# An early load of the exp table and an order guard for score steps, in a fused attention and gated-MLP kernel

## The chip, the cores and the metric

The kernel runs on one core of a Trainium2 chip. The metric is the device time of one execution in microseconds (us).

The core has a matrix engine (TensorE; PE in the profile, PEld for its weight loads), a vector engine (VectorE, DVE), an engine for activation functions and copies (ScalarE, ACT), a general engine (GpSimd, POOL), and SyncE (SP), which here issues most of the DMAs (transfers between memories).

## The reference, cut to what matters

Two layers run on the same normalised input, and both are added to it: a sliding-window attention (2048 tokens, 32 heads of 16, window 256) and a gated MLP whose gate mixes tokens with a 2048 x 2048 matrix.

```python
xn = layernorm(x)
# A: attention over a window
qkv = xn @ wqkv
scores = einsum('bhqd,bhkd->bhqk', q, k) * 16 ** -0.5     # masked to 0 <= i - j < 256
o = softmax(scores) @ v
A = o @ wo
# B: gated MLP
z = gelu(xn @ w_in);  z1, z2 = halves of z
g = w_sp @ layernorm(z2) + b_sp                            # mixes tokens
B = (z1 * g) @ w_out
return x + A + B
```

## The kernel before

It has two phases. Phase one computes `z` (a gelu on ScalarE) and 39 of 48 "QKV units", each four matmuls into one PSUM bank (PSUM is the memory that this kernel's matmuls write into) and one copy out of it. Phase two does the other nine QKV units, and then interleaves on TensorE: score steps (`S`), token mixing (`gf`), attention times V (`o`) and the output projections (`fo`). ScalarE takes the exp of each score step. The order of phase two is made at build time by a small loop that keeps estimates of the time on each engine; each engine gets its own list of instructions in that order.

The end of phase one:

```python
    for n in range(NB):
        ...                              # z_half(n, 0), z_half(n, 1) with gelu, and 3 QKV units
    r = z_stats(NB - 1)
    z_apply(NB - 2, r)
    z_apply(NB - 1, r)
    nc.vector.tensor_copy(out=b_all[:], in_=b_bf[:])
```

The loop of phase two:

```python
while ...:
    now = est["pe"]
    if si < len(groups):
        gk, us_ = groups[si]
        if not qq and not s_third and kind != "q" and q_end + 0.3 <= now:
            third_s()                    # QKV's PSUM banks become a third score buffer
        free = set_end[2 * si - (2 if s_third else 1)] + 0.1 if si >= 1 else 0.0
        if free <= now and not qq and (us_[-1] < NE or pv_done > us_[-1] - NE):
            end = do_scores(gk, us_)     # score matmuls, and their exps on ScalarE
            ...
            continue
    ...
    if cur is None:
        cur, kind = pick()               # "q": the next QKV unit, while there are any
    c = next(cur)                        # issues one matmul of the current work
    ...
```

`qq` is empty as soon as the last QKV unit has been picked, so a score step may be issued in the middle of that unit.

A V unit is copied to a staging tile and scattered by four DMAs, all issued by SyncE:

```python
    st = stg.tile([P, 2, H // 2, DH], BF, name="vst", bufs=3)
    (nc.vector.tensor_copy if n % 2 else nc.scalar.copy)(out=st[:], in_=...)
    for e in range(2):
        for kk in range(2):
            nc.sync.dma_start(out=v_bd[e * KB : (e + 1) * KB, v_at(2 * n + kk, e), :, :],
                              in_=st[kk * KB : (kk + 1) * KB, e, :, :])
```

The exps go into three large tiles `E` in turn. The first two have their own space; the third takes the space of the QKV pools, which close first:

```python
def e_tile(u):
    i = u % NE                           # NE = 3
    if i not in E_sb:
        E_sb[i] = Et = (ep if i < 2 else late()).tile([P, EW], BF, ...)   # late() closes the QKV pools
        nc.vector.memset(Et[...], 0.0)   # two memsets of the columns between the rows
```

The softmax here doesn't subtract the row's maximum and nothing guards it: scores larger than these inputs give would overflow.

Of the kernel before, what the change touches and what calls it, by code (L numbers as in the profile page):

```python
# [11 lines left out]
ACT = mybir.ActivationFunctionType  # L12
# [29 lines left out]
def kernel(  # L42
# [12 lines left out]
    nc = tc.nc  # L55
# [18 lines left out]
    warm = pers.tile([P, 8], F32, name="warm")  # L74
# [62 lines left out]
    def load_wsp(t):  # L137
        wspT[t] = wspp.tile([P, NB, P], BF, name="wspT")
        nc.sync.dma_start_transpose(out=wspT[t][:], in_=B_w_sp[t * P : (t + 1) * P, :])
# [14 lines left out]
    with ExitStack() as actx:  # L154
# [23 lines left out]
        with nc.allow_non_contiguous_dma(reason="tiny bias gather"):  # L178
# [3 lines left out]
            out=w_out_sb[:, 0:5, :], in_=B_w_out[0:640, :].rearrange("(c p) n -> p c n", p=P)  # L182
# [31 lines left out]
        def setup_late():  # L214
            mt = lt.tile([P, 2, P], BF, name="mt", bufs=1)
            nc.gpsimd.memset(mt[:], 1.0)
            nc.gpsimd.affine_select(
                out=mt[:, 0, :], in_=mt[:, 0, :], pattern=[[1, P]], compare_op=ALU.is_ge,
                fill=0.0, base=0, channel_multiplier=-1,
            )  # L220
            nc.gpsimd.affine_select(
                out=mt[:, 1, :], in_=mt[:, 1, :], pattern=[[-1, P]], compare_op=ALU.is_gt,
                fill=0.0, base=0, channel_multiplier=1,
            )
            for i in range(3):
                for e in range(2):
                    r = slice(e * KB, (e + 1) * KB)
                    nc.gpsimd.tensor_copy(out=mACA[r, i, :], in_=mt[r, i % 2, r])
# [11 lines left out]
        def rstd(mvt, k):  # L240
            ve = sm.tile([P, 4], F32, name="ve")
            rs = sm.tile([P, 4], F32, name="rs")
            nc.vector.tensor_scalar(  # L243
                out=ve[:, 0:k], in0=mvt[:, 0:k, 1], scalar1=LN_EPS, scalar2=None, op0=ALU.add
            )
            nc.gpsimd.tensor_tensor(  # L246
                out=rs[:, 0:k], in0=ve[:, 0:k], in1=mhalf[:, 0:k], op=ALU.pow
            )
            return rs

        def ln_batch(b0, k):
            mvt = sm.tile([P, 4, 2], F32, name="mvt")
            for n in range(b0, b0 + k):
                ln_stats(n, b0, mvt)
                if n == b0 + k - 1:
                    rs = rstd(mvt, k)
                    for m in range(b0, b0 + k):
                        rsx[m] = rs[:, m - b0 : m - b0 + 1]
                yield
# [10 lines left out]
        def transposes(n, xn):  # L270
            if n >= 8:
                nc.sync.dma_start_transpose(out=xnT[:, :, n * P : (n + 1) * P], in_=xn[:])
                return
            tp = psum["f"].tile([P, NC, P], BF, name="tp", tag="f")
            for c in range(NC):
                nc.tensor.transpose(  # L276
                    out=tp[:, c, :], in_=xn[:, c * P : (c + 1) * P], identity=ident[:]
                )
            nc.scalar.copy(out=xnT[:, :, n * P : (n + 1) * P], in_=tp[:])  # L279

        def z_half(n, half):
            zp = ps_s.tile([P, 2, 512], F32, name="zp", tag="S")
            for c in range(NC):
                for j in range(2):
                    f0 = half * FH + j * HALF
                    nc.tensor.matmul(  # L286
                        zp[:, j, 0:HALF],
                        lhsT=xnT[:, c, n * P : (n + 1) * P],
                        rhs=w_in_sb[:, c, f0 : f0 + HALF],
                        start=(c == 0), stop=(c == NC - 1),  # L290
                    )
            dst = (z1 if half == 0 else z2n)[:, n, :]
            nc.scalar.activation(  # L293
                out=dst.rearrange("p (j f) -> p j f", j=2),
                in_=zp[:, :, 0:HALF], func=ACT.Gelu_apprx_tanh,
            )
# [3 lines left out]
        def z_stats(n):  # L300
            if n % 2 == 0:
                zmv[n // 2] = sm.tile([P, 4, 2], F32, name="zmv")
            mvt = zmv[n // 2]
            st = sm.tile([P, 2, nc.vector.BN_STATS_DIM], F32, name="st2")
            for j in range(2):
                nc.vector.bn_stats(out=st[:, j, :], in_=z2n[:, n, j * HALF : (j + 1) * HALF])
            nc.vector.bn_aggr(out=mvt[:, n % 2, :], in_=st[:])
            if n % 2 == 1:
                return rstd(mvt, 2)
            return None  # L310
# [24 lines left out]
        for n in range(NB):  # L335
            b, j = divmod(n, 4)
            z_half(n, 0)
            if n == 0:
                transposes(1, xns.pop(1))
            elif n == 6:  # L340
                setup_late()
            elif n in (9, 10):
                load_wsp(n - 9)
            if b < 3:
                if j < 2:
                    for _ in ln_batch(4 * b + 4 + 2 * j, 2):
                        pass
                if 1 <= j < 3:
                    for m in range(2):
                        k = 4 * b + 4 + 2 * (j - 1) + m  # L350
                        xns[k] = ln_apply(k)
                        if k >= 8:
                            transposes(k, xns.pop(k))
            if n >= 1:
                r = z_stats(n - 1)
                if r is not None:
                    z_rs[n - 1] = r
            if n >= 3:
                for _ in qkv_unit(*qkv_list.pop(0)):
                    pass  # L360
            z_half(n, 1)
            if n == 0:
                transposes(2, xns.pop(2))
            elif n == 1:
                transposes(3, xns.pop(3))
                setup_early()
            if n % 2 == 1 and n >= 3:
                r = z_rs[n - 2]
                z_apply(n - 3, r)
                z_apply(n - 2, r)  # L370
            if n >= 3:
                for _ in range(2):
                    for _ in qkv_unit(*qkv_list.pop(0)):
                        pass
            if b == 0 and j >= 2:
                for m in range(2):
                    k = 4 + 2 * (j - 2) + m
                    transposes(k, xns.pop(k))
        r = z_stats(NB - 1)
        z_apply(NB - 2, r)  # L380
        z_apply(NB - 1, r)
# [5 lines left out]
    def third_s():  # L387
        o_ctx.close()
        psum.pop("o")
        s_third.append(  # L390
            ctx.enter_context(tc.tile_pool(name="ps_s3", bufs=1, space=bass.MemoryType.PSUM))
        )
# [255 lines left out]
    qq = list(qkv_list)  # L648
# [3 lines left out]
    cur = None  # L652
# [24 lines left out]
    kind = None  # L677
    while si < len(groups) or mask_q or pv_q or qq or gq or fq or cur is not None:
# [3 lines that stand above are left out]
            if not qq and not s_third and kind != "q" and q_end + 0.3 <= now:  # L682
                third_s()
            free = set_end[2 * si - (2 if s_third else 1)] + 0.1 if si >= 1 else 0.0
            if free <= now and not qq and (
                us_[-1] < NE or pv_done > us_[-1] - NE
            ):
                end = do_scores(gk, us_)
                if gk != "R1":
                    for u in us_:  # L690
                        mask_q.append((end + 0.1, (u, gk), (gk in "TQ") == (u % 2 == 0)))
                si += 1
                continue
        while mask_q and mask_q[0][0] <= now:
            t0, m, fin = mask_q.pop(0)
            dur = do_mask(*m)
            est["dve"] = max(est["dve"], t0) + dur
            if fin:
                pv_q.append((est["dve"] + 0.2, divmod(m[0], NG)))
        if cur is None:  # L700
            if evac[-4 if qq else -2] + 0.1 > now:
                est["pe"] = now + 0.05
                continue
            cur, kind = pick()
            if cur is None:
                est["pe"] = now + 0.05
                continue
        c = next(cur)
        if c > 0:
            est["pe"] += c  # L710
        else:
            evac.append(-c)
            est["pe"] += 0.1
            if kind == "q":
                q_end = max(q_end, -c)
            if kind == "pv":
                pv_done += 1
            if kind == "f":
                f_done += 1
            cur = None  # L720
# [27 lines left out]
```

## Time and profile before

| | value |
|---|---|
| median time, 20 runs | 274.36 us (273.38 to 276.06) |
| span in the profile | 271.9 us |
| TensorE busy | 264.3 us, 97% |
| ScalarE busy | 198.9 us, 73% |

The page of the kernel before: the span, the busy time of each engine, and the engines' shares of the chain of work that ended last.

```profile
span 271.9 us, 8363 instructions
...
PE 264.3 (97%) x3565; PEld 160.7 (59%) x3565; DVE 153.9 (57%) x421; ACT 198.9 (73%) x268; POOL 35.8 (13%) x80
...
PE 92%; DMA 3%; ACT 1%; DVE 1%; SPq 1%; issue 0%; ACTq 0%
```

TensorE does nearly everything on the chain. A busy share of 97% says that little idle time is left to win, and says nothing of where it lies. So look for holes. Adding up the gaps between TensorE's records gives 3.07 us in the first 20 us, 1.05 us between 80 and 92 us, and none after that. The hole between 80 and 92 us is where phase one becomes phase two. The view of waits names it (who waited for what: us in total, times, longest):

```profile
PE S L592 <- ACT E_1139 L613: 0.9, 2, 0.6
```

TensorE in order of time there (start, duration, engine, line, operation, tiles, count, idle time and what ended it):

```profile
77.58 1.33 PE L286 MATMUL zp<-w_in_sb,xnT 128*128 128x344 bf16 x8
...
87.67 0.38 PE L100 MATMUL pj_f<-xnT,wqkv 128*128 128x512 bf16 x1
87.98 0.37 PE L592 MATMUL S<-qT,kpad 32*128 32x192 bf16 x8
88.28 0.82 PE L100 MATMUL pj_f<-xnT,wqkv 128*128 128x512 bf16 x3
88.94 1.48 PE L468 MATMUL gf<-z2n,wspT 128*128 128x344 bf16 x9
90.73 0.20 PE L592 MATMUL S<-qT,kpad 32*128 32x64 bf16 x2 [0.32 <-ACT E_1139 L613]
91.54 0.34 PE L592 MATMUL S<-qT,kpad 32*128 32x64 bf16 x14 [0.60 <-ACT E_1139 L613]
91.82 1.34 PE L468 MATMUL gf<-z2n,wspT 128*128 128x344 bf16 x8
```

Read it downwards. 77.58 is the last group of matmuls for `z`; **this moment is called z0 below**. At 87.67 the last QKV unit has issued one matmul, then score step 0 is pushed in (87.98), then come the other three. Score step 1 should follow nine `gf` matmuls at about 90.3. Its first two matmuls wait until 90.73 and the rest until 91.54, each for an exp. ScalarE in the same window tells why:

```profile
87.87 0.59 ACT L106 CAST qT<-pj_o 128x512 bf16<-128x512 f32 x1 [1.39 <-PE pj_o L100]
88.47 1.28 ACT L613 ACT_TABLE_LOAD   x1
89.76 1.73 ACT L613 ACTIVATE E_1139<-S 128x896 bf16<-128x896 f32 x2
91.38 0.59 ACT L109 CAST kst<-pj_f 128x512 bf16<-128x512 f32 x1
...
94.37 0.92 ACT L613 ACTIVATE E_1142<-S 128x896 bf16<-128x896 f32 x1
95.27 0.92 ACT L613 ACTIVATE E_1322<-S 128x896 bf16<-128x896 f32 x1
```

The first exp finds the gelu table loaded. The load takes 1.28 us and pushes both exps back, and the copy of the last K unit (`kst`) stands behind them. Line 95.27 is the first exp into the third E tile (`E_1322`). VectorE, at that time, prepares this tile:

```profile
94.94 0.27 DVE L419 MEMSET E_1322<- 128x256 uint32 x1 [0.65 <-DMA v_bd<-vst]
```

That memset had waited for the last V scatter DMA, which landed at 94.73.

### The profile page before, as it was taken

To read this page: it belongs to the slowest core of one execution; us is meant where nothing else is said; L and a number is where in the kernel's file an instruction comes from. 1 tells how busy PE (TensorE), PEld (TensorE's weight loads), DVE (VectorE), ACT (ScalarE), POOL (GpSimd) and SP (SyncE) were. 2 spreads that over 40 slices of the span, in tenths; PEclk is the share of its full clock that TensorE was granted. 3 is DMA by queue.
4 is the path that set the end of the run, shared out by engine and by line. 5 is a ranking of instruction groups with operands and counts; after the bars stand their busy time and mean duration, and the time that the engine had idled before them with its cause. 6 is when DMAs were issued, how large, how long until landed. Compare 5 with 4: busy or idle time off the path is not lost.

```text
span 271.9 us, 8363 instructions
## 1 busy us (share of the span) xinstructions
PE 264.3 (97%) x3565; PEld 160.7 (59%) x3565; DVE 153.9 (57%) x421; ACT 198.9 (73%) x268; POOL 35.8 (13%) x80
## 2 busy tenths in 40 slices
PE   6899999999999899999999999999999999999994
PEld 2665555555554466666665675757566666766651
DVE  7796947945456365646545555665556465522222
ACT  7576565565564999999999999999999999200000
POOL 6222412101101011010101010101010101101110
PEclk9999999999999999999999999999999999999999
DMA  7983231664201248462909276539162448456621
GB/s 231 389 214 118 59 67 32 119 84 105 45 21 32 48 68 169 96 132 50 140 12 176 45 108 78 110 33 154 40 150 44 105 70 119 101 116 145 145 70 59
DMA packets 73078, 27.84 MB, mean 102 GB/s; under 512 B 62944, under 2 KB 71568, under 8 KB 73040
## 3 DMA queue, kind: packets, MB, share of 16 engines
q1 hardware_dynamic: 71312, 23.10, 43.9%
q0 software_dynamic: 1440, 3.93, 4.8%
q8 instruction: 28, 0.46, 0.7%
q10 hardware_dynamic: 288, 0.26, 0.3%
q14 instruction: 10, 0.08, 0.1%
HBM read 8.41 MB, written 2.10 MB: 39 GB/s over the span
## 4 chain that ended last, share of the span: by engine, by line
PE 92%; DMA 3%; ACT 1%; DVE 1%; SPq 1%; issue 0%; ACTq 0%
PE gf L468 28%; PE o L539 14%; PE zp L286 13%; PE fo L496 8%; PE S L592 6%; PE fo L502 5%; PE pj_f L100 4%; PE pj_o L100 4%; DMA w_in_sb<-in_B_w_in_dram 3%; PE pj_f L119 2%; PE pj_o L119 2%; DMA v_bd<-vst 1%; ACT E_1139 L613 1%; PE tp L276 0%; SPq L162 0%; DVE xo L507 0%
## 5 line engine op out<-in xcount | busy, mean ns | idle before, releaser
L468 PE MATMUL gf<-z2n,wspT 128*128 128x344 bf16 x512 | 84.9, 310 | 0.0
L468 PEld LDWEIGHTS <-wspT 128*128 128x128 bf16 x512 | 46.0, 97 | 25.5 <-issue 2.4
L286 PE MATMUL zp<-w_in_sb,xnT 128*128 128x344 bf16 x256 | 42.2, 309 | 1.4 <-DMA w_in_sb<-in_B_w_in_dram 1.4
L474 DVE SCALAR_TENSOR_TENSOR u<-gf,b_all,z_61 128x344 bf16<-128x344 f32 x32 | 18.4, 576 | 38.7 <-PE gf L468 31.3
L613 ACT ACTIVATE E_1142<-S 128x1024 bf16<-128x1024 f32 (+3 forms) x43 | 36.5, 871 | 0.3
L613 ACT ACTIVATE E_1139<-S 128x1024 bf16<-128x1024 f32 (+3 forms) x43 | 35.4, 848 | 0.1
L286 PEld LDWEIGHTS <-xnT 128*128 128x128 bf16 x256 | 24.9, 98 | 16.7 <-ACT xnT L279 0.8
L613 ACT ACTIVATE E_1322<-S 128x1024 bf16<-128x1024 f32 (+3 forms) x39 | 33.6, 923 | 0.2
L592 PE MATMUL S<-qT,kpad 32*128 32x256 bf16 (+3 forms) x648 | 30.1, 230 | 0.9 <-ACT E_1139 L613 0.9
L509 POOL DMA_DIRECT2D out_dram<-xo x14 | 7.7, 548 | 146.8 <-DVE xo L507 146.8
L592 PEld LDWEIGHTS <-kpad 32*128 32x128 bf16 x960 | 14.1, 92 | 18.3 <-issue 17.4
L496 PE MATMUL fo<-w_out_sb,uT 128*128 128x512 bf16 x96 | 24.4, 379 | 0.0
L111 DVE TENSOR_SCALAR kpad<-kst,hmask 128x512 bf16<-128x512 bf16 x32 | 9.8, 350 | 24.7 <-ACT kst L109 24.6
L507 DVE TENSOR_TENSOR xo<-fo,xo 128x512 bf16<-128x512 f32 x16 | 11.1, 692 | 22.0 <-PE fo L502 22.0
L246 POOL TENSOR_TENSOR rs<-ve,mhalf 128x2 f32<-128x2 f32 (+1 forms) x18 | 12.4, 689 | 64.7 <-DVE ve L243 64.7
L293 ACT ACTIVATE z2n<-zp 128x688 bf16<-128x688 f32 x16 | 11.9, 745 | 11.1 <-PE zp L286 11.1
L293 ACT ACTIVATE z_61<-zp 128x688 bf16<-128x688 f32 x16 | 11.9, 746 | 10.9 <-PE zp L286 10.9
L100 PEld LDWEIGHTS <-wqkv 128*128 128x128 bf16 x128 | 12.4, 98 | 11.8 <-issue 0.2
L619 DVE TENSOR_TENSOR E_1142<-E_1142,mACA 128x512 bf16<-128x512 bf16 (+1 forms) x32 | 15.3, 504 | 4.9 <-ACT E_1142 L613 4.7
L502 PE MATMUL fo<-wo_sb,oT 128*128 128x512 bf16 x64 | 17.3, 380 | 0.0
L100 PE MATMUL pj_f<-xnT,wqkv 128*128 128x512 bf16 x64 | 16.6, 379 | 0.0
L619 DVE TENSOR_TENSOR E_1139<-E_1139,mACA 128x512 bf16<-128x512 bf16 (+1 forms) x31 | 14.5, 496 | 3.6 <-ACT E_1139 L613 3.5
(225 smaller groups left out, 372.4 us busy)
## 6 DMA issues: line engine op xcount, KB each, us to landing
v_bd<-vst SPq DMA_DIRECT2D x64, 32.0 KB, 1.9
xo<-in_A_x_dram POOLq DMA_DIRECT2D x16, 128.0 KB, 3.3
out_dram<-xo POOLq DMA_DIRECT2D x14, 128.0 KB, 2.8
wqkv<-in_A_wqkv_dram SPq DMA_DIRECT2D x1, 1536.0 KB, 11.3
w_in_sb<-in_B_w_in_dram SPq DMA_DIRECT2D x2, 688.0 KB, 6.3
w_out_sb<-in_B_w_out_dram SPq DMA_DIRECT2D x1, 640.0 KB, 6.2
xt_101<-in_A_x_dram SPq DMA_DIRECT2D x1, 512.0 KB, 7.9
xt_102<-in_A_x_dram SPq DMA_DIRECT2D x1, 512.0 KB, 12.1
```

The lines of the kernel that those rows point to most:

```text
L100: nc.tensor.matmul(pt[:], lhsT=wqkv[:, c, w0 : w0 + P], rhs=xnT[:, c, t0 : t0 + 512], start=(c == 0), stop=(c == NC - 1),)
L246: nc.gpsimd.tensor_tensor(out=rs[:, 0:k], in0=ve[:, 0:k], in1=mhalf[:, 0:k], op=ALU.pow)
L286: nc.tensor.matmul(zp[:, j, 0:HALF], lhsT=xnT[:, c, n * P : (n + 1) * P], rhs=w_in_sb[:, c, f0 : f0 + HALF], start=(c == 0), stop=(c == NC ...
L293: nc.scalar.activation(out=dst.rearrange("p (j f) -> p j f", j=2), in_=zp[:, :, 0:HALF], func=ACT.Gelu_apprx_tanh,)
L468: nc.tensor.matmul(gf[:, 0:HALF], lhsT=wspT[t][:, c, :], rhs=z2n[:, c, j * HALF : (j + 1) * HALF], start=(c == 0), stop=(c == NB - 1),)
L474: nc.vector.scalar_tensor_tensor(out=u[:, j * HALF : (j + 1) * HALF], in0=gf[:, 0:HALF], scalar=b_all[:, t : t + 1], in1=z1[:, t, j * HALF ...
L496: nc.tensor.matmul(fo[:], lhsT=uTs[t][:, ch, :], rhs=w_out_sb[:, ch, :], start=(ch == 0), stop=False,)
L502: nc.tensor.matmul(fo[:], lhsT=oTs[t][:, c, :], rhs=wo_sb[:, c, :], start=False, stop=(c == NC - 1),)
L539: nc.tensor.matmul(o[:, q, s, :], lhsT=Et[:, col : col + P], rhs=v_bd[:, v_at(kb, 0) : v_at(kb, 1) + 1 : kb + 1, 4 * G + s, :], start=(i = ...
L592: nc.tensor.matmul(S[s // 2][:, s % 2, col : col + n * KB], lhsT=kpad[32 * s : 32 * s + 32, G, kb, :, :].rearrange("p e k -> p (e k)"), rh ...
L613: nc.scalar.activation(out=dst, in_=src, func=ACT.Exp, scale=SM_SCALE)
L619: nc.vector.tensor_tensor(out=ap, in0=ap, in1=m.unsqueeze(1).to_broadcast([P, ap.shape[1], 2, KB]), op=ALU.mult,)
```

## The change

The intent: load the exp table while ScalarE has time, directly behind the last gelu, by an exp of four numbers that nobody uses; and let no score step into a QKV unit that is being issued, so that ScalarE's copy for that unit isn't put behind exps.

```diff
@@ end of phase one @@
+        nc.scalar.activation(out=warm[:, 0:4], in_=warm[:, 4:8], func=ACT.Exp)
         r = z_stats(NB - 1)
@@ the loop of phase two @@
-            if free <= now and not qq and (
+            if free <= now and not qq and (cur is None or kind != "q") and (
                 us_[-1] < NE or pv_done > us_[-1] - NE
             ):
```

The built kernels differ on TensorE in one place only: the eight matmuls of score step 0 stand behind the last unit's four instead of behind its first. On ScalarE the load and the dummy exp come after a V copy, and the last K copy comes before the first exps. As the loop's estimates moved too, the third score buffer opens one step earlier, at step 1. From there to the end the order of TensorE's work is the same.

## The prediction

> **What bounds the kernel now.** TensorE: 264.3 of 271.9 us busy, 92% of the chain that ended last (page, parts 1 and 4). From 92 us on it never idles (gaps between its records: 3.07 us in the first 20 us, 1.05 from 80 to 92, then none). ScalarE is 9 tenths full from 92 to 236 us, but follows: score steps find their buffer freed 0.15 to 0.6 us earlier, and exps start 0.03 to 0.25 us after the scores end (timeline). So only the hole at the transition can be saved.
>
> **That hole (timeline, 79 to 99 us).** Score step 0 stands after the first matmul of the last QKV unit. ScalarE reaches it at 88.47: exp table load 1.28 us, two exps from 89.76, then the last K copy (91.38). Step 1 needs both score buffers, as the third is not open yet: TensorE idles 0.32 us at 90.41 and 0.60 at 90.94 (wait view: S on E_1139, 0.9); against back-to-back issue, 0.39 + 0.80 = 1.19 us.
>
> **What the change does (instruction order of the built kernels).** (a) Table load and dummy exp (the pair took 1.28 + 0.21 us for gelu at the start) move to about 81.3 us, behind a V copy. Two copies end 1.3 us later, at about 83.3 and 83.9; their PSUM banks are wanted at 83.9 and 84.8, and VectorE takes the K copy only at 84.71: no cost. No later load remains. The Trainium skill ("ScalarE: Activation LUTs", What ACT_TABLE_LOAD costs) gives 1283 ns plus a 1380 ns drain; this trace shows the 1283 but no drain: the copy before ends at 88.46, the exp starts at 89.76. (b) Step 0 follows the last unit's four matmuls, so the K copy precedes the exps, and the third score buffer opens one step earlier. TensorE's order is otherwise identical to the end. First exp about 89.26 (0.5 earlier); step 1 no longer waits; TensorE gains 1.19 us by 91.
>
> **Where most is lost.** Step 3's exp writes the third E tile, in the QKV pool's space. Its memset waits for the last V scatter DMA: twelve are issued from 85.92 to 93.43 (0.63 us each), the last lands at 94.73; memset 94.94 to 95.21, exp 95.27. ScalarE's wait there ended at 95.22, so this gate already binds, and the change leaves it: the V copy that starts the twelve is held on VectorE until 85.20 by other work. ScalarE will be ready about 94.0 and idle 1.2 us; step 4's scores need the buffer freed at 96.2, so TensorE stalls 0.6 to 0.7 us. Left: about 0.5 us, kept to the end, since TensorE then runs the same order without waits.
>
> **Predicted:** 273.9 us (before 274.44), 8 in 10 between 272.9 and 274.8. Faster by over 2%: 1%; within 2%: 98%; slower: 1%.
>
> **Signs that it is right.** Table load near 81.3 us, no new TensorE gap at 83 to 86; first exp near 89.3 behind the K copy; no gap before step 1; a new ScalarE gap of 1.2 us before the first E_1323 exp, released by the memset, still at 95.2 to 95.3; a TensorE gap of 0.6 us before step 4; span 0.5 us shorter.
>
> **What would make it wrong.** If the V scatter lands earlier, or the exp doesn't wait for the memset, the gain is up to 1.2 us. If the delayed copies hold a bank, or later steps wait for ScalarE, it goes to zero. The spread of runs (273.6 to 275.8) exceeds the gain.

## The result

| | before | after |
|---|---|---|
| median | 274.36 us (20 runs) | 273.63 us (272.80 to 274.95, 10 runs) |
| ratio | | 0.9972, 95% interval 0.9952 to 0.9992 |

A ratio is the mean time of one kernel's fast runs over that of the other's of the same rounds, so it isn't quite the ratio of the medians. It stands for about 0.8 us, with an interval of 0.2 to 1.3 us (0.0028 x 274.36, and the same for the ends of the interval). The measured time lies in the predicted range.

Now compare the profiles. The page after:

```profile
span 272.0 us, 8364 instructions
...
PE 264.3 (97%) x3565; PEld 160.6 (59%) x3565; DVE 153.8 (57%) x421; ACT 198.5 (73%) x269; POOL 35.7 (13%) x80
...
PE 90%; DMA 4%; DVE 2%; ACT 1%; SPq 1%; issue 0%; POOL 0%; DVEq 0%; ACTq 0%; POOLq 0%
```

The span is 0.1 us *longer*, though the kernel is faster. The profile is of one execution, and this one began badly. The chain of waits before and after, from its first microseconds (start, duration, what):

```profile
2.25 7.01 DMA w_in_sb<-in_B_w_in_dram
```

```profile
2.23 8.10 DMA w_in_sb<-in_B_w_in_dram
```

The same first load of `w_in` took 8.10 us instead of 7.01. Neither part of the change touches it. TensorE's phase one then runs late by the same 1.07 us at every point compared: z0 is at 78.65 instead of 77.58. So spans can't be compared here, but times from z0 can. TensorE after:

```profile
78.65 1.33 PE L286 MATMUL zp<-w_in_sb,xnT 128*128 128x344 bf16 x8
...
88.72 1.03 PE L100 MATMUL pj_f<-xnT,wqkv 128*128 128x512 bf16 x4
89.68 0.37 PE L593 MATMUL S<-qT,kpad 32*128 32x192 bf16 x8
89.99 1.49 PE L469 MATMUL gf<-z2n,wspT 128*128 128x344 bf16 x9
91.41 0.20 PE L593 MATMUL S_1252<-qT,kpad 32*128 32x64 bf16 x2
...
91.69 1.34 PE L469 MATMUL gf<-z2n,wspT 128*128 128x344 bf16 x8
...
96.57 0.20 PE L593 MATMUL S_1371<-qT,kpad 32*128 32x64 bf16 x2
96.85 0.20 PE L593 MATMUL S<-qT,kpad 32*128 32x64 bf16 x2
...
97.14 0.76 PE L540 MATMUL o<-v_bd,E_1143 128*128 128x48 bf16 x24
```

ScalarE after:

```profile
82.35 1.28 ACT L379 ACT_TABLE_LOAD   x1
83.64 0.21 ACT L379 ACTIVATE warm<-warm 128x4 f32<-128x4 f32 x1
...
89.83 0.59 ACT L109 CAST kst<-pj_f 128x512 bf16<-128x512 f32 x1 [0.32 <-PE pj_f L100]
90.31 1.74 ACT L614 ACTIVATE E_1140<-S 128x896 bf16<-128x896 f32 x2
...
94.20 1.01 ACT L614 ACTIVATE E_1143<-S_1286 128x896 bf16<-128x896 f32 x1
95.88 1.73 ACT L614 ACTIVATE E_1323<-S 128x896 bf16<-128x896 f32 x2 [0.67 <-DMA v_bd<-vst]
```

Subtract z0 and set the two beside each other. This table was worked out from the two traces:

| us from z0 | before | after |
|---|---|---|
| exp table load starts | 10.89 | 3.70 |
| first exp | 12.18 | 11.66 |
| first `gf` matmul, after step 0 | 11.36 | 11.34 |
| `gf` after step 1 | 14.23 | 13.04 |
| `gf` after step 3 | 17.53 | 16.34 |
| last V scatter has landed | 17.15 | 17.13 |
| first exp into the third E tile | 17.68 | 17.23 |
| `o` after step 4 | 19.40 | 18.49 |
| last matmul of the kernel | 190.49 | 189.61 |
| end of the span | 194.29 | 193.40 |

The change wins 1.19 us at step 1, as predicted, and loses about 0.3 us of that at step 4. The rest, 0.88 us, is kept to the last matmul: from 101 us on, TensorE's records of the two traces stand at one constant distance. The 0.89 us at the end agrees with the 0.8 us of the timed runs.

VectorE after, the memset of the third E tile:

```profile
95.98 0.27 DVE L420 MEMSET E_1323<- 128x256 uint32 x1 [1.82 <-DMA v_bd<-vst]
```

Compare it with ScalarE's list: the exp into that tile started at 95.88, 0.10 us *before* the memset. The chain of waits of the kernel after says directly who released the exp:

```profile
93.88 1.90 DMA v_bd<-vst
...
95.80 0.04 ACTq L614
...
95.88 0.93 ACT E_1323 L614
...
96.85 0.20 PE S L593 x2
```

The scatter lands, ScalarE's queue passes its wait, the exp runs, and the score matmuls of step 4 that need its buffer start at 96.85. The memset has no part in this chain. This is where the prediction went astray.

### The profile page after: what moved, and what is told of

Its sections match the earlier page's. It is cut to its first block, busy times and chain, and to the rows that moved or that the text cites. A ratio compares the mean times of both kernels' runs of the same rounds, so it can differ in the third digit from the quotient of the medians.

```text
span 272.0 us, 8364 instructions
## 1 busy us (share of the span) xinstructions
PE 264.3 (97%) x3565; PEld 160.6 (59%) x3565; DVE 153.8 (57%) x421; ACT 198.5 (73%) x269; POOL 35.7 (13%) x80
## 4 chain that ended last, share of the span: by engine, by line
PE 90%; DMA 4%; DVE 2%; ACT 1%; SPq 1%; issue 0%; POOL 0%; DVEq 0%; ACTq 0%; POOLq 0%
PE gf L469 27%; PE o L540 14%; PE zp L286 13%; PE fo L497 8%; PE S L593 6%; PE fo L503 5%; PE pj_f L100 4%; PE pj_o L100 4%; DMA w_in_sb<-in_B_w_in_dram 3%; PE pj_f L119 2%; PE pj_o L119 2%; DMA v_bd<-vst 1%; ACT E_1140 L614 1%; PE tp L276 0%; SPq L130 0%; ACT kst L109 0%
## 5 line engine op out<-in xcount | busy, mean ns | idle before, releaser
L593 PE MATMUL S<-qT,kpad 32*128 32x192 bf16 (+3 forms) x640 | 29.9, 231 | 0.1
L100 PE MATMUL pj_o<-xnT,wqkv 128*128 128x512 bf16 x64 | 16.4, 379 | 0.0
```

The costliest lines, as they stand in the source:

```text
L100: nc.tensor.matmul(pt[:], lhsT=wqkv[:, c, w0 : w0 + P], rhs=xnT[:, c, t0 : t0 + 512], start=(c == 0), stop=(c == NC - 1),)
L593: nc.tensor.matmul(S[s // 2][:, s % 2, col : col + n * KB], lhsT=kpad[32 * s : 32 * s + 32, G, kb, :, :].rearrange("p e k -> p (e k)"), rh ...
```

## The experiments

The theory after the first comparison had three parts. (1) The hole at step 1 came from the table load standing ahead of the first exps, and nothing else. The rival: the order guard, which lets step 1 use the third score buffer, removes the hole. (2) The 0.3 us lost at step 4 come from the landing of the last V scatter. The rivals: ScalarE's own pace, or the memset. (3) Before the change this gate didn't bind.

Each run was timed in five rounds beside the kernel before and profiled once. Six runs of each kernel can't resolve 0.3 us, so the verdicts rest on times from z0 in the traces. How far those can be trusted is seen where nothing should differ: the first `gf` after step 0 stands at 11.34 to 11.36 in the first seven traces of the table, and the last matmul at 190.49 in the two traces of `before` and e4. A late z0 doesn't spoil them: the profiled run of e5 came with a granted clock of 0.991 (the share of its full clock that TensorE was given) and its z0 is at 79.96, and its last matmul still stands at 189.30, as in e3.

| us from z0 | before | after | e1 dummy exp only | e2 guard only | e3 after, 6 DMAs moved | e4 before, 6 moved | e5 after, 8 moved | e6 e5 + memsets moved | e7 after, V units first |
|---|---|---|---|---|---|---|---|---|---|
| first exp | 12.18 | 11.66 | 10.79 | 13.08 | 11.67 | 12.18 | 11.66 | 11.87 | 11.39 |
| first `gf` | 11.36 | 11.34 | 11.35 | 11.34 | 11.34 | 11.35 | 11.34 | 11.54 | 11.06 |
| `gf` after step 1 | 14.23 | 13.04 | 13.04 | 14.33 | 13.04 | 14.23 | 13.04 | 13.24 | 12.76 |
| last V scatter landed | 17.15 | 17.13 | 17.13 | 17.14 | 13.50 | 13.48 | 14.98 | 14.70 | 13.05 |
| exp into third E | 17.68 | 17.23 | 17.23 | 17.80 | 16.49 | 17.68 | 16.48 | 16.69 | 16.21 |
| `o` after step 4 | 19.40 | 18.49 | 18.49 | 19.51 | 18.20 | 19.39 | 18.20 | 18.40 | 17.92 |
| last matmul | 190.49 | 189.61 | 189.62 | 190.60 | 189.30 | 190.49 | 189.30 | 189.50 | 189.02 |
| end | 194.29 | 193.40 | 193.40 | 194.37 | 193.85 | 195.04 | 193.48 | 193.70 | 192.78 |

| | median | before, same rounds | ratio | 95% interval |
|---|---|---|---|---|
| e1 | 273.86 | 274.43 | 0.9984 | 0.9963 to 1.0005 |
| e2 | 274.44 | 274.43 | 0.9997 | 0.9981 to 1.0014 |
| e3 | 273.74 | 274.43 | 0.9979 | 0.9954 to 1.0004 |
| e4 | 275.23 | 274.43 | 1.0024 | 1.0004 to 1.0044 |
| e5 | 273.47 | 274.41 | 0.9972 | 0.9941 to 1.0002 |
| e6 | 273.97 | 274.41 | 0.9998 | 0.9966 to 1.0030 |
| e7 | 272.73 | 274.41 | 0.9944 | 0.9911 to 0.9978 |

All seven gave correct results. Part of the spread of times goes with the granted clock: the two slowest runs of e6 (275.09 and 275.32 us) had 0.994 of it, its other four (273.70 to 274.15 us) 0.997 to 1.000.

### e1: the dummy exp alone

```diff
+        nc.scalar.activation(out=warm[:, 0:4], in_=warm[:, 4:8], func=ACT.Exp)
         r = z_stats(NB - 1)
```

> The dummy exp alone; score step 0 stays inside the last QKV unit. Measured from the start of the last group of z matmuls (call it z0) the span to the end was 194.29 us before and 193.40 with the whole change. Theory (the stall came from the table load standing ahead of the first exps): the exps start at about z0+10.9 instead of 12.18, both score buffers are free when step 1 comes, TensorE has no gap there, and the span from z0 is about 193.4 to 193.5, so the whole gain. Rival (the third score buffer, opened one step earlier by the order guard, removes the stall): step 1 still waits for the second exp, and the span from z0 is 193.9 or more.

ScalarE and TensorE of e1:

```profile
88.71 1.73 ACT L614 ACTIVATE E<-S 128x896 bf16<-128x896 f32 x2
...
95.15 5.80 ACT L614 ACTIVATE E<-S 128x896 bf16<-128x896 f32 x9 [0.73 <-DMA v_bd<-vst]
```

```profile
90.68 0.35 PE L593 MATMUL S<-qT,kpad 32*128 32x64 bf16 x16
```

The exps follow the scores at once (88.71, z0 + 10.79), and step 1 issues its 16 matmuls in one piece with no wait, although it has only the two old score buffers (the build loop of e1, replayed, opens the third at step 2, as the one of the kernel before does). The span from z0 is 193.40 us, that of the whole change. So the dummy exp is the whole gain. The second line of ScalarE shows the same gate as in the kernel after: its exps run out and it waits for the scatter.

### e2: the order guard alone

```diff
-            if free <= now and not qq and (
+            if free <= now and not qq and (cur is None or kind != "q") and (
```

> The order guard alone; the table load stays ahead of the first exp. Theory: the last K copy goes first (about z0+11.2), then the load (1.28 us), so the first exp starts near z0+13.0; step 1 waits until about z0+13.9, as before, and the span from z0 stays within 0.15 us of 194.29. Rival (third buffer): step 1 needs only one exp, and the span from z0 falls to about 193.4 to 193.7.

ScalarE and TensorE of e2:

```profile
90.39 1.28 ACT L613 ACT_TABLE_LOAD   x1
91.69 9.03 ACT L613 ACTIVATE E<-S 128x896 bf16<-128x896 f32 x15
```

```profile
91.36 0.20 PE L592 MATMUL S<-qT,kpad 32*128 32x64 bf16 x2
92.66 0.34 PE L592 MATMUL S<-qT,kpad 32*128 32x64 bf16 x14 [1.09 <-ACT E L613]
```

The third buffer lets the first two matmuls of step 1 start at 91.36; the other 14 wait 1.09 us for the first exp, which the load has pushed to 91.69. In all, 194.37 us from z0: 0.08 us more than before. The rival has fallen: the guard alone gains nothing, and with the dummy exp (e1 against the whole change) it adds nothing that the traces show.

### e3 and e4: half of the last scatter issued by another engine

```diff
-                    nc.sync.dma_start(
+                    (nc.gpsimd if e and n >= 13 else nc.sync).dma_start(
                         out=v_bd[e * KB : (e + 1) * KB, ...
```

e3 has this on the kernel after, e4 on the kernel before. The scatter is slow because SyncE issues the last twelve DMAs one by one, 0.63 us apart. "DMA: Bandwidth & Descriptors" in the Trainium skill (section "Issuing engines are not separate DMA queues") says that issuing from several engines saves only the sequencer's time. That is just what is short here.

> The whole change, and of the last twelve V scatter DMAs the second halves (six) are issued from the GpSimd queue. Theory (what is left of the stall, 0.3 us of 1.19, is lost because the first exp into the third E tile waits for the last V scatter to land, z0+17.13): the last lands before z0+16, that exp starts at about z0+16.3 when ScalarE is ready, score step 4 has no gap, and the span from z0 is about 193.1. Rival (ScalarE's own pace, or the memset, holds it): the span from z0 stays 193.4.

> The kernel before with the same split of the V scatter. Theory: before the change the exp into the third E tile was released by its scores (z0+17.6), not by the scatter, so nothing is gained: span from z0 within 0.1 us of 194.29. If the prediction's reading was right, that the memset behind the scatter already bound there, the exp would start earlier and the span would fall by 0.1 us or more.

With six DMAs each on two queues, the last one landed at z0 + 13.50 instead of 17.13. ScalarE and TensorE of e3:

```profile
90.15 9.95 ACT L614 ACTIVATE E<-S 128x896 bf16<-128x896 f32 x16
```

```profile
96.41 0.35 PE L593 MATMUL S<-qT,kpad 32*128 32x64 bf16 x16
```

ScalarE runs 16 exps in one unbroken row, the one into the third E tile at z0 + 16.49, 0.08 us after the matmuls of its scores end (16.41). So without the gate the scores release it. Step 4 issues all its 16 matmuls in one piece. The last matmul starts at 189.30, 0.31 us earlier than in the kernel after: all of the 1.19 us is now kept. In e4 the scatter landed at 13.48, and the memset moved up too; VectorE of e4, whose z0 is 78.41:

```profile
95.11 0.27 DVE L419 MEMSET E<- 128x256 uint32 x1
```

That is 16.70 instead of 17.36, and yet the exp started at 17.68 and the last matmul at 190.49, both as before. So the gate didn't bind before the change, be it the landing or the memset; there the exp waited for its scores, whose matmuls end at 17.59 in e4.

Yet the end of e3 came at 193.85, later than without the split, and e4 was slower than before. The expectation of the end had failed in both. The traces show where: SyncE closes the program by a list of waits, one after another. Start in us after the last matmul's, of those waits and of the barrier behind them:

```
after:  1.53 1.60 1.67 1.74 1.81 2.20 2.29 2.35 2.87   barrier 3.04   (output lands at 2.85)
e3:     1.52 1.59 2.86 2.93 3.01 3.08 3.15 3.22 3.60   barrier 3.82   (output lands at 2.85)
```

In both, the last output lands 2.85 us after the last matmul. In the kernel after the wait for it is the last in the list. In e3 it is the third, and the other six come after it (the next expectation says seven), 0.07 us apart with one longer step. Six DMAs fewer on SyncE had moved the output to another semaphore.

### e5: eight DMAs moved instead of six

```diff
-                    nc.sync.dma_start(
+                    (nc.gpsimd if n == 15 or e and n >= 13 else nc.sync).dma_start(
```

> As the split run of before on the whole change, but eight of the last twelve scatter DMAs go to the GpSimd queue instead of six. In that run TensorE's last matmul started 0.31 us earlier (z0+189.30 against 189.61), yet the span from z0 ended 0.45 us later, as the closing waits of SyncE, which stand in a fixed order, met the last output's landing early in their list and had seven more to go through. With eight DMAs moved, the last output falls on the same semaphore as before. Theory: last matmul at z0+189.3 and end at about z0+193.1 (before 194.29, change 193.40). Rival (moving DMAs to GpSimd lengthens the end by itself): end near z0+193.8 again.

The last matmul is at 189.30 again. The wait for the output is the last in the list again, but the barrier comes at 3.45 instead of 3.04 us after the last matmul, and the end at 193.48. The expected 193.1 is missed by 0.4 us. So the order of the waits was part of the loss, and another part stays. GpSimd's closing drain grew from 3.27 us (no scatter DMAs) to 3.58 (six) and 3.75 (eight), but it ended 2.6 us before the barrier, so it isn't shown to be the cause. The trace does show where most of the 0.4 us lies. Behind the wait for the output SyncE has two drains; they start at 2.94 and 3.30, against 2.94 and 3.01 in the kernel after, and the second takes 0.13 us instead of 0.01. This is the longer step of the lists above: in all nine traces one step of 0.35 to 0.39 us stands directly before SyncE's 208th instruction. With 216 instructions on SyncE (kernel after) it lies at 1.81 to 2.20, before the output lands, and costs nothing; with 213 (e3) or 211 (e5) it comes after the landing. Why that instruction is late stays open.

### e6: the memsets of the first two E tiles on GpSimd

```diff
-            nc.vector.memset(Et[...], 0.0)             # both memsets of e_tile
+            (nc.gpsimd if i < 2 else nc.vector).memset(Et[...], 0.0)
```

The target was another small hole. In every trace so far the last V unit (the expectation calls it the second last) starts about 0.3 us late (before: 85.94, where back-to-back issue would give 85.65): it needs the PSUM bank that a V copy on VectorE frees late.

> As the run before it, and the four memsets of the first two E tiles (0.62 us of VectorE, standing ahead of the K copies and of the V copy that TensorE waits for at z0+8.1) go to GpSimd. Theory: the 0.28 us by which the second last V unit starts late, in the kernel before and in the change alike, goes too: last matmul at z0+189.0, end at about z0+192.8, so 1.5 us less than before. If that wait has another cause, no change against the run before it.

A miss: the last matmul came 0.2 us *later* than in e5. VectorE and GpSimd of e6:

```profile
84.04 1.63 DVE L313 TENSOR_SCALAR z2n<-z2n,zmv,rs 128x688 bf16<-128x688 bf16 x2 [0.87 <-POOL rs L246]
```

```profile
83.94 0.52 POOL L420 MEMSET E<- 128x512 bf16 x1
...
84.96 0.15 POOL L424 MEMSET E<- 128x64 bf16 x1
```

The two instructions on VectorE took 1.63 us; in the kernel after they took 0.83:

```profile
84.32 0.83 DVE L313 TENSOR_SCALAR z2n<-z2n,zmv,rs 128x688 bf16<-128x688 bf16 x2 [0.87 <-POOL rs L246]
```

Taken singly, the first took 1.27 us instead of 0.46 and ended at 85.30, just after GpSimd's last memset (85.11); the second, behind the memsets, took 0.44. The Trainium skill ("SBUF — State Buffer", section "Who interferes with whom") says that VectorE and GpSimd share a port pair, and that VectorE's `tensor_scalar` can enter a mode in which one of the two blocks until the other is done. The times fit that, but no run shows the mode itself, so the cause is argued: what the trace shows is that work taken off VectorE's list came back as a longer instruction on it.

### e7: the V units of the last block first

```diff
-    qkv_list = [(b, i) for b in range(4) for i in (0, 1, 8, 2, 3, 9, 4, 5, 10, 11, 6, 7)]
+    qkv_list = [(b, i) for b in range(3) for i in (0, 1, 8, 2, 3, 9, 4, 5, 10, 11, 6, 7)]
+    qkv_list += [(3, i) for i in (8, 9, 10, 11, 0, 1, 2, 3, 4, 5, 6, 7)]
@@ copy of a V unit @@
-            (nc.vector.tensor_copy if n % 2 else nc.scalar.copy)(
+            (nc.vector.tensor_copy if n % 2 and n < 15 else nc.scalar.copy)(
```

This is on top of the whole change. It starts the scatter earlier instead of sharing it out, and leaves every DMA on SyncE.

> The whole change, and the four V units of the last token block stand first in their block instead of in between; the last one is copied by ScalarE. All scatter DMAs stay on SyncE, so the closing order stays. Theory: the last scatter lands by about z0+14 and no V copy waits behind the memsets, so both the 0.31 us at score step 4 and the 0.28 us at z0+8.1 go: last matmul about z0+189.0, end about z0+192.8. Rival: the other order of units makes a projection wait for its PSUM bank, and a new gap of 0.3 us or more appears between z0+4 and z0+11.

All came as expected. The first `gf` is 0.28 us earlier than in the kernel after, the last scatter lands at z0 + 13.05, and step 4 runs in one piece:

```profile
95.51 0.35 PE L594 MATMUL S<-qT,kpad 32*128 32x64 bf16 x16
```

The last matmul is at 189.02 (expected 189.0) and the end at 192.78 (expected 192.8), 1.51 us less than before. Timed, it is 272.73 against 274.41 us, a ratio of 0.9944, which is 1.5 us. This version beats the kernel before. It wasn't timed beside the kernel after; in the traces it is 0.62 us shorter from z0 (192.78 against 193.40).

## Why the prediction was right, and where it was wrong

- **The hole and its cause: right.** 1.19 us predicted at step 1, 1.19 measured (14.23 to 13.04). e1 and e2 show that the table load's place is the cause. The prediction listed the guard's effects beside it as if they shared in the gain; e1 shows that they weren't needed.
- **The load costs nothing at its new place: right.** It started at z0 + 3.70 (82.35, or 81.28 at the pace of the other trace; predicted 81.3), and TensorE reached the first `gf` at 11.34, as before.
- **A part of the gain is lost at the third E tile: right in kind, wrong in size.** The step that failed reads "ScalarE's wait there ended at 95.22, so this gate already binds": the prediction took the gate to be the memset (ending at 95.21) behind the scatter. The kernel after starts that exp 0.10 us before the memset, and 0.10 us after the scatter's landing. What had ended ScalarE's wait in the kernel before was its scores, whose matmuls end at 95.19; e4, where the scatter landed 3.7 us earlier and the exp started at the same 17.68, shows it. So does ScalarE's queue, whose last wait before that exp ends at 17.64 in the kernel before and at 17.63 in e4. A coincidence of 0.02 us had been read as a cause, though the exp depended on the landing and on its scores.
- **So two terms of the sum were off.** The gate stood at z0 + 17.23 instead of 17.69. The idle time of ScalarE before it was 0.7 us (exp at 17.23; without the gate, in e3, at 16.49) and not 1.2, and the stall of TensorE at step 4 was 0.3 us (18.49 against 18.20 in e3) and not 0.6 to 0.7. Hence 1.19 - 0.3 = 0.9 us in place of the 0.5 predicted.
- **The gain is kept to the end: right.** 0.88 us at the last matmul, 0.91 just after step 4.
- **Within 2%, 273.9 us: right.** It was 273.63. The prediction's range held the gain of 0.5 as well as that of 0.9, and the median alone couldn't have told the two apart.

## What to carry to other kernels

Put a table switch where the engine has slack, by a dummy call behind the last use of the old table: one line was worth the whole gain here, and the reordering that went with it nothing. When two events fall within a few hundredths of a microsecond, nearness isn't proof of who released whom; look at what the instruction waits for, and move one of the two. To see less than 1% in one profiled execution, count from a moment behind the noisy start: the spans differed by +0.1 us, the times from z0 by -0.89.

## What the Trainium skill lacked or had wrong

- "ScalarE: Activation LUTs", section "What ACT_TABLE_LOAD costs", gives about 1283 ns for a load and another 1380 ns for a drain with every switch. Here the load took 1.28 us in every trace, but no drain was to be seen: in the kernel before the copy ahead of it ends at 88.46, the load starts at 88.47, and the exp starts at 89.76. A switch cost 1.3 us, not 2.7.
- "DMA: Bandwidth & Descriptors", section "Issuing engines are not separate DMA queues", calls the time saved by issuing from several engines usually small relative to the DMA. Here it wasn't small: twelve DMAs of 32 KB were issued 0.63 us apart and each landed about 1.9 us after its issue, and with half of them on a second engine the last one landed 3.6 us earlier.
- No page that was read tells of SyncE's closing list of waits. Which semaphore the last output falls on decided how many 0.07 us steps came after its landing, and the number of SyncE's instructions whether one step of 0.35 to 0.39 us did: the barrier stood at 3.04 us after the last matmul (kernel after), at 3.45 (e5) or at 3.82 (e3).
